# Moving the third round of decays and the third group of tiles behind the first inversion in a fused RWKV-7 and hash-routing kernel

## The chip, the cores and the metric

The kernel runs on one core of one Trainium2 chip. The metric is the device time of one execution in microseconds (us). A core has a matrix engine (PE, with its weight loads shown as PEld), a vector engine (DVE), an activation engine (ACT), a general engine (POOL), and SyncE (SP), which here only issues DMAs. Each engine works through its own queue in order.

## The reference

The first block is a recurrent attention (RWKV-7) over 4 batches, 8 heads, 768 steps and a head size of 40. The second block sends each of the 3072 resulting rows (320 wide) to one of 8 experts, chosen by a hash of its token id.

```python
for t in range(S):                      # B, H, S, D = 4, 8, 768, 40
    y[:, :, t] = einsum('bhd,bhde->bhe', r[t], state)
    Sa = einsum('bhde,bhe->bhd', state, a[t])
    state = state * w[t][:, :, None, :] - einsum('bhd,bhe->bhde', Sa, b[t])
    state = state + einsum('bhd,bhe->bhde', v[t], k[t])
x = y.transpose(0, 2, 1, 3).reshape(B * S, H * D)
expert = token_ids * 2654435761 % 8
for e in range(8):                      # w1: 320x1024, w2: 1024x320
    out[expert == e] = maximum(x[expert == e] @ w1[e], 0) @ w2[e]
```

## The kernel before

**The work.** The sequence is cut into 12 chunks of 64 steps. A *tile* is one chunk of two batches, so there are 24 tiles, numbered u = 0 to 23; tiles u and u + 2 are the same batches and hang together through the state. Everything is float32.

- `decays(ri, ...)` makes the running products of `w` for one *round* of two chunks, which is four tiles: round ri serves tiles 4ri to 4ri + 3, and there are 6 rounds. It loads `wt` (L352), multiplies up a tree (`todo`, L363/L366, DVE), joins the halves by a small matmul `f_ps` (L382, PE), and spreads products and reciprocals down the tree (`then`, L389 to L377, DVE). The results `pb` and `qb` are stored to DRAM by 8 DMAs on SP (L337); tiles read them back as `pl` and `ql` through POOL's queue (L458, L460). Round 0 is turned on DVE and read without that detour.
- `tile_a(u)` loads `al` and `kb` (inputs a, b, k; SP, L308), forms `at` and `z` (DVE, L473 and L477), transposes them (`z_ps` L491 and `t_ps` L528 on PE, copied by ACT) and makes the scores `a_ps` (PE). ACT copies the part to be inverted to `pk` and `no`; DVE masks the rest into `mk` (L521).
- `group_i(gi, ...)` inverts the scores of four tiles at once, on DVE alone: POOL clears `nu` (L546), DVE transposes `pk` into it (L552), then runs 30 pairs of `outer` (L570) and `nu` (L577), and transposes the result into `ut` (L585, L586). There are six groups; "inversion 0" is that of tiles 0 to 3.
- `tile_m(u)` finishes the inverse on PE and ACT (`x_ps`, `u_ps`), and `tile_b(u)` does the recurrent part: `r0` and `r1` (`r_ps`), `nc`, `x_t`, `s` (state update, DVE `st`), `sd`, `rc` (DVE mask `mr`, L700), and `y` (DVE `xs`, L736), which POOL stores to `x_rows` (L740).
- `routing()` sorts the tokens to experts, in 30 small steps; the expert part (L1003 `up_ps`, L1021 `dn_ps`) follows when all tiles are done.

**The order.** The queues of PE, DVE, ACT and POOL are written out by hand. Each piece is given a *tick*; all pieces are sorted by tick and issued in that order, so a tick is a place in the queue and not a time. `tile_a(u)` stands at tick u, `tile_m(u)` at u + 7, `tile_b(u)` at u + 8 (`LAG = 8`), its `y` at u + 9. Within a tick the steps follow the list `STEPS`, a step being 1/14 of a tick. Inversion gi starts behind the scores of its last tile (tick 4gi + 3.8) and must be done at tick 4gi + 7.2, just before `tile_m` of its first tile. SP's queue is not in that list (`manual_schedule(engines={PE, DVE, Activation, Pool})`): the framework orders the DMAs issued there.

Buffers limit how early a load may start: `al`, `kb`, `pl`, `ql` have two each, `wt` one. A load into a buffer that is still being read holds up whatever stands behind it in its queue.

Of the kernel before, what the change touches and what calls it, by code (L numbers as in the profile page):

```python
# [36 lines left out]
F32 = mybir.dt.float32  # L37
# [10 lines left out]
def kernel(  # L48
# [55 lines left out]

    col = const.tile([P, P], I32)
    nc.gpsimd.iota(col[:], pattern=[[1, P]], base=0, channel_multiplier=0)
    row = const.tile([P, P], I32)
# [14 lines left out]


    FH = F // 2
    early = pool("early", 1)

    def load_w1(t, e, dma):

# [36 lines left out]
    plan = []  # L165


    STEPS = ["r0", "r1", "z", "y", "nc", "x", "at_t", "x_t", "s", "u", "sd", "a", "r_t", "rc"]

    def at_tick(tick, step=None, order=0):  # L170
        if step is not None:
# [83 lines left out]
    def half(i):  # L255
        return slice(i * C, (i + 1) * C)
# [58 lines left out]
    def decays(ri, t_w, t0, span, t_f, span_f=None, stores=None):  # L315
# [28 lines left out]

        @at_tick(t_w)
        def _():
            x["w"] = wt = early.tile([P, HC * D], F32, tag="wt", name="wt")

            dma = (nc.sync.dma_start, nc.scalar.dma_start if ri < 2 else nc.sync.dma_start)
            for y in range(2 * RN):  # L350
                src = w.rearrange("b h (n t) e -> (b h) n (t e)", t=HC)[:, ri * 2 * RN + y]
                dma[y % 2](wt[y * BH:(y + 1) * BH], src)  # L352
# [87 lines left out]
    def of_batches(rows, b0, n):  # L440
        return rows[:, b0 * H:(b0 + n) * H, :].rearrange("t bh e -> t (bh e)")

    def tile_a(u):

        n, g = divmod(u, NG)
        ri, rn = divmod(n, RN)
        x = tiles[u]

        @at_tick(u - 1.7)
        def _():  # L450
            x["p"] = pl = work.tile([P, DM], F32, tag="pl", name="pl")
            x["a"] = al = work.tile([P, DM], F32, tag="al", name="al")
            x["q"] = ql = work.tile([P, 2, DM], F32, tag="ql", name="ql")
            x["kb"] = kb = work.tile([P, 2, DM], F32, tag="kb", name="kb")
            p_rows, q_rows = ((rounds[0][i].rearrange("t (bh e) -> t bh e", e=D) if ri == 0 else pq_dram[ri]["pq".index(i)])
                              [rn * C:(rn + 1) * C] for i in "pq")
            for be in range(2):
                nc.gpsimd.dma_start(pl[half(be)], of_batches(p_rows, 2 * g + be, 1))  # L458
            for be in range(2):
                nc.gpsimd.dma_start(ql[half(be)], of_batches(q_rows, 2 * g, 2))  # L460
            load(lambda be, rows: by_head(al, rows), a, 2 * g, n * C)
# [5 lines left out]
        late = {4: 0.45, 5: 0.3, 6: 0.15}.get(u, 0.0)  # L467

        @at_tick({0: -0.6, 1: -0.4, 2: 0.45, 3: 1.45}.get(u, u + late - (0.1 if late else 0.6)))
        def _():  # L470
            x["at"], x["z"] = at_r(u), z_r(u)

            nc.vector.scalar_tensor_tensor(wide(x["at"]), by_head(x["a"]), -1.0, by_head(x["p"]), op0=OP.mult, op1=OP.mult)  # L473

            def view(t):
                return t.rearrange("p b (hp two e) -> p (b hp) two e", hp=HP, two=2)
            nc.vector.tensor_tensor(heads(x["z"].rearrange("p b hp x -> p (b hp) x")), view(x["kb"][:]), view(x["q"][:]),  # L477
                                    op=OP.mult)

        @at_tick(u + late, "at_t")  # L480
        def _():
            x["at_t"] = t = work.tile([P, HP, 2, C], F32, tag="at_t", name="at_t", bufs=LAG)
            turn(t, x["at"])

        @at_tick(u + late, "z")
        def _():
            x["z_t"] = t = z_t
            p = two_banks("z_ps")
            for be in range(2):
                for hp in range(HP):  # L490
# [46 lines left out]
    def group_i(gi, t0, t1, t2):  # L537
# [22 lines left out]
        for j in range(1, BLK - 1):  # L560

            m = BLK - 1 - j
            full = [P, j // 2 + 1, m, 2]
            n = full[1] * m * 2

            @at_tick(t1 + dt * (2 * j - 1), order=9)
            def _(j=j, full=full, n=n):
                x["t"] = work.tile([P, BLK * BLK // 4 + BLK // 2], F32, tag="outer", name="outer")
                tv = x["t"][:, 0:n].rearrange("p (c i k) -> p c i k", c=full[1], k=2)
                nc.vector.tensor_tensor(tv, paired(x["u"])[:, 0:full[1], j:j + 1, :].to_broadcast(full),  # L570
                                        paired(x["n"])[:, j // 2, j + 1:, j % 2].unsqueeze(1).unsqueeze(3).to_broadcast(full),
                                        op=OP.mult)
# [72 lines left out]
    def tile_b(u, t0):  # L645
# [2 lines left out]
        last = n == NCH - 1  # L648
        st, sb, sd = st_r(g), sb_r(g), sd_r(g)

        @at_tick(t0, "r0")
        def _():
            x["r1_ps"] = p = bank([P, DM], "r1_ps").rearrange("p (two x e) -> p two x e", two=2, e=D)
            for _, be, hp in heads_of("hq", "be", "al"):
                mm(p[half(al(hp)), :, hp % HQ * 2 + be, :], x["at_t"][:, hp, be, :], sb[:, be, hp],
                   start=be == 0 and hp % HQ == 0, stop=False)
# [97 lines left out]
    t_a = STEPS.index("a") / len(STEPS)  # L754

    decays(0, -4.0, -3.0, 0.4, -2.5, 0.3)
    decays(1, -2.15, -1.9, 0.4, (-0.55, -0.54, -0.53, -0.35, -0.34, -0.3, -0.29, 0.2), stores=1.34)
    decays(2, -0.25, 0.87, 0.45, (1.87, 1.9, 1.91, 2.0, 2.01, 2.1, 2.11, 2.2), stores=3.34)
    for ri in range(3, NR):
        t0 = ri * RN * NG - 5.0  # L760
        decays(ri, t0 - 1.0, t0 + 0.25, 1.0, t0 + 1.3, 1.1)
    for u in range(NU):
        tile_a(u)
        tile_s(u, u + LAG)
        tile_m(u, u + LAG)
# [13 lines left out]
    def routing():  # L779
# [4 lines left out]
        for b_ in range(B):  # L784
# [475 lines left out]
```

## Time and profile before

| what | value |
|---|---|
| median of 3 runs | 657.6 us (655.33 to 657.83) |
| the profiled execution: time / span | 660.41 us / 658.5 us |
| busy: PE, DVE, ACT, POOL | 560.7, 349.4, 295.0, 194.8 us |
| start of inversion 0 and end of its last transpose | 57.5 and 93.8 us |
| end of inversions 1, 2, 3, 4, 5 | 143.7, 205.3, 257.6, 309.6, 360.3 us |
| start of the expert part | 410.0 us |
| mean granted PE clock | 0.946 |

The time of an execution is 1.9 us above its span. The expert part from 410 us on is untouched by the diff. The page's second part cuts the span into 40 slices of 16.5 us; each digit is a busy share in tenths.

### The profile page before, as it was taken

Reading aid. Unit: us, or ns where it says so; the run is one execution under the profiler, and the core shown is the slowest. Engines: PE = TensorE matmul, PEld = TensorE weight load, DVE = VectorE, ACT = ScalarE, POOL = GpSimd, SP = SyncE. Lnnn points to the kernel's source line nnn. Section 1 sums busy time; section 2 is a strip of 40 time slices with the busy share of each in tenths; the row PEclk is TensorE's granted clock in tenths of the full one; section 3 lists DMA queues with packets and bytes.
Section 4 is the critical chain, followed back from the end, with each engine's and each line's share of the span. In section 5 each row is a group of like instructions: output and inputs, shape, how many; then the busy total and the mean of one; then the engine's idle time right before and its main releaser. Section 6 shows DMA issues by size and latency. Waiting matters only on the chain.

```text
span 658.5 us, 22965 instructions
## 1 busy us (share of the span) xinstructions
PE 560.7 (85%) x9866; PEld 427.1 (65%) x9866; DVE 349.4 (53%) x920; ACT 295.0 (45%) x695; POOL 194.8 (30%) x327
## 2 busy tenths in 40 slices
PE   0244559979998999999979998999999999999995
PEld 0233447868887887888868877775665646565653
DVE  6766968957868996796698723133020302113010
ACT  4133447757776677768746662113131313101110
POOL 0503341325343343533312330173404131212101
PEclk9967669979999999999997998999999999999999
DMA  5999996878598787842422640869243364131000
GB/s 90 203 174 170 180 185 119 162 152 158 117 192 153 142 166 140 184 96 54 98 51 50 162 106 17 275 216 313 74 144 117 104 219 143 38 101 40 30 11 24
DMA packets 195770, 85.13 MB, mean 129 GB/s; under 512 B 176718, under 2 KB 186191, under 8 KB 195664
## 3 DMA queue, kind: packets, MB, share of 16 engines
q1 hardware_dynamic: 184208, 46.25, 36.5%
q0 software_dynamic: 11264, 36.72, 19.3%
q8 instruction: 78, 1.28, 0.8%
q10 hardware_dynamic: 192, 0.66, 0.4%
q14 instruction: 28, 0.23, 0.1%
HBM read 66.54 MB, written 15.40 MB: 124 GB/s over the span
## 4 chain that ended last, share of the span: by engine, by line
PE 44%; issue 22%; DVE 19%; DMA 6%; POOL 4%; ACT 3%; SPq 1%; POOLq 0%; DVEq 0%; ACTq 0%
PE up_ps L1003 6%; PE dn_ps L1021 6%; PE y_ps L289 4%; DVE nu L577 3%; PE s_ps L289 3%; DVE outer L570 3%; PE a_ps L289 3%; PE r_ps L289 3%; PE x_t_ps L688 3%; PE rc_ps L289 2%; POOL out_dram L1026 2%; PE t_ps L528 2%; DVE mr L700 2%; PE z_ps L491 2%; PE nc_ps L289 2%
## 5 line engine op out<-in xcount | busy, mean ns | idle before, releaser
L1011 DVE TENSOR_SCALAR ht<-up_ps 128x416 f32<-128x416 f32 (+2 forms) x36 | 19.4, 543 | 165.0 <-PE up_ps L1008 163.4
L1021 PE MATMUL dn_ps<-w,ht 128*128 128x320 f32 x336 | 91.7, 433 | 0.0
L1003 PE MATMUL up_ps<-xt,w 128*128 128x416 f32 x224 | 81.3, 516 | 0.0
L1021 PEld LDWEIGHTS dn_ps<-w,ht 128*128 128x128 f32 x336 | 63.3, 190 | 25.5
L1026 POOL DMA_INDIRECT out_dram<-o,idx_all x26 | 26.1, 1006 | 166.5 <-ACT o L1025 160.4
L740 POOL DMA_DIRECT2D x_rows<-xs x44 | 23.3, 534 | 171.5 <-DVE xs L736 101.5
L1003 PEld LDWEIGHTS up_ps<-xt,w 128*128 128x128 f32 x224 | 41.9, 190 | 36.9 <-issue 31.7
L570 DVE TENSOR_TENSOR outer<-nu 128x252 f32<-128x252 f32 (+8 forms) x180 | 63.3, 352 | 4.6
L577 DVE TENSOR_TENSOR nu<-nu,outer 128x252 f32<-128x252 f32 (+8 forms) x180 | 63.4, 352 | 4.3
L1013 ACT ACTIVATE ht<-up_ps 128x416 f32<-128x416 f32 (+2 forms) x36 | 17.2, 479 | 107.4 <-PE up_ps L1008 107.4
L1025 ACT COPY o<-dn_ps 128x320 f32<-128x320 f32 x26 | 11.1, 425 | 92.0 <-PE dn_ps L1021 92.0
L491 PE MATMUL z_ps<-ident,z 128*104 128x128 f32 x192 | 32.8, 326 | 20.7 <-DVE z L477 17.5
L493 ACT COPY z_t<-z_ps 104x512 f32<-104x512 f32 x48 | 25.8, 589 | 54.8 <-PE z_ps L491 54.8
L491 PEld LDWEIGHTS z_ps<-ident,z 128*104 128x104 f32 x192 | 25.6, 155 | 23.5 <-issue 18.3
L458 POOL DMA_DIRECT2D pl<-p_rows x48 | 25.3, 532 | 52.2 <-DVE at L473 21.5
L678 ACT COPY x<-nc_ps 64x320 f32<-64x320 f32 x48 | 20.2, 420 | 38.9 <-PE nc_ps L289 38.4
L289 PE MATMUL a_ps<-at_t,z_t 64*64 64x64 f32 x1536 | 30.9, 233 | 7.5 <-ACT at_t L529 7.3
L700 DVE TENSOR_TENSOR mr<-rc_ps,after 128x1024 f32<-128x1024 f32 x24 | 29.3, 1219 | 14.9 <-PE rc_ps L289 14.8
L289 PEld LDWEIGHTS a_ps<-at_t,z_t 64*64 64x64 f32 x1536 | 27.3, 145 | 12.8 <-ACT at_t L529 9.8
L289 PE MATMUL rc_ps<-r_t,x_t 64*64 64x64 f32 x1536 | 30.2, 226 | 5.1 <-issue 4.4
L289 PE MATMUL y_ps<-z,mr 128*64 128x40 f32 x768 | 27.3, 231 | 7.2 <-DVE mr L700 6.8
L289 PEld LDWEIGHTS rc_ps<-r_t,x_t 64*64 64x64 f32 x1536 | 26.2, 138 | 10.0 <-issue 6.4
(227 smaller groups left out, 1123.9 us busy)
## 6 DMA issues: line engine op xcount, KB each, us to landing
ql<-q_rows POOLq DMA_DIRECT2D x48, 160.0 KB, 5.2
w<-in_moe_w_dram SPq DMA_DIRECT2D x10, 640.0 KB, 6.9
w<-in_moe_w_dram SPq DMA_DIRECT2D x10, 512.0 KB, 4.5
al<-in_a_dram SPq DMA_DIRECT2D x48, 80.0 KB, 4.4
kb<-in_b_dram SPq DMA_DIRECT2D x48, 80.0 KB, 3.8
kb<-in_k_dram SPq DMA_DIRECT2D x48, 80.0 KB, 3.9
pl<-p_rows POOLq DMA_DIRECT2D x48, 80.0 KB, 4.2
r<-in_r_dram SPq DMA_DIRECT2D x48, 80.0 KB, 3.6
```

The costliest lines, as they stand in the source:

```text
L289: nc.tensor.matmul(out_, lhsT=lhsT, rhs=rhs, start=start, stop=stop, skip_group_check=True)
L458: nc.gpsimd.dma_start(pl[half(be)], of_batches(p_rows, 2 * g + be, 1))
L491: nc.tensor.transpose(p[0:R, be, hp * P:(hp + 1) * P], x["z"][:, be, hp, :], ident[:])
L493: nc.scalar.copy(t[0:R, be].rearrange("p h t -> p (h t)"), p[0:R, be])
L570: nc.vector.tensor_tensor(tv, paired(x["u"])[:, 0:full[1], j:j + 1, :].to_broadcast(full), paired(x["n"])[:, j // 2, j + 1:, j % 2].unsque ...
L577: nc.vector.tensor_tensor(o, o, x["t"][:, 0:n].rearrange("p (c i k) -> p c i k", c=full[1], k=2), op=OP.add)
L678: nc.scalar.copy(x["x"][half(be), be].rearrange("p (a q) (two e) -> p a (q two) e", a=2, two=2)[:, :, :, 0:D], p[half(be), :, 0:HP * D].re ...
L700: nc.vector.tensor_tensor(t[:].rearrange("p two h t -> p (two h) t"), p[:].rearrange("p two (h t) -> p (two h) t", t=C), after[:].unsqueez ...
L740: dma(x_of[2 * g + be, n * C:(n + 1) * C], xs[half(be), :])
L1003: nc.tensor.matmul(p[:], lhsT=w1[c][:, (f0 + i) * P:(f0 + i + 1) * P], rhs=xt[:, c, 0:n], start=(c == 0), stop=False)
L1021: nc.tensor.matmul(p[i * m:(i + 1) * m], lhsT=ht[:, f, c0:c0 + m], rhs=w2[f // (FP // 2)][:, f % (FP // 2), :], start=(f == 0), stop=(f == ...
L1026: st = nc.gpsimd.indirect_dma_start(out=out[:], out_offset=bass.IndirectOffsetOnAxis(ap=idx, axis=0), in_=o[0:m], in_offset=None, bounds_c ...
```

## The change

- **Order of the rounds and tiles.** `t_of(u)` gives the tick of `tile_a(u)`. Tiles 4 to 6 stay late by 0.45, 0.3 and 0.15 as before. Tiles 8 to 11 move from ticks 8 to 11 to ticks 10.4, 10.85, 11.3 and 11.75; tiles 12 and 13 move by 0.5 and 0.2. Inversion gi begins behind the scores of its last tile at the new tick and is due at the same tick as before, so inversion 2 begins at 12.6 and not at 11.9.
- **Decays.** Round 2 is computed at ticks 7.2 to 8.1 (before: 0.87 to 2.2), round 3 at 8.6 to 10.4 (before: 7.25 to 9.4). `wt` has two buffers, and the loads of rounds 1, 3, 4 and 5 are issued earlier (4 and 5 by 1.6 ticks).
- **First inputs.** `al` and `kb` have a piece of their own. For tiles 0 to 3 it stands at ticks -3.9 to -2.7; tiles 2 and 3 borrow the buffers of `x_t`, `mr` and `py`, which are not needed before tick 8.
- **`r0`** of the next tile moves from the head of a tick to between `r_t` and `rc` at its end, just behind the scores.
- **Room.** `outer` has one buffer in place of two; `row` and the temporaries of `routing()` share buffers that are free by then.
- **Routing.** The last steps are spread over ticks 27.25 to 30.3 (before: 27.35 to 29.1), and the first two gathers move from tick 29.2 to 30.5.

```diff
-    STEPS = ["r0", "r1", "z", "y", "nc", "x", "at_t", "x_t", "s", "u", "sd", "a", "r_t", "rc"]
+    STEPS = ["r1", "z", "y", "nc", "x", "at_t", "x_t", "s", "u", "sd", "a", "r_t", "r0", "rc"]
...
-            x["w"] = wt = early.tile([P, HC * D], F32, tag="wt", name="wt")
+            x["w"] = wt = early.tile([P, HC * D], F32, tag="wt", name="wt", bufs=2)
...
+    LATE = {4: 4.45, 5: 5.3, 6: 6.15}
+    CLOSE = {8: 10.4, 9: 10.85, 10: 11.3, 11: 11.75}
+    AFTER = {12: 12.5, 13: 13.2}
+
+    def t_of(u):
+        return {**LATE, **CLOSE, **AFTER}.get(u, u)
...
-        @at_tick(u - 1.7)
+        ta, close = t_of(u), u in CLOSE
+        @at_tick(ta - 1.7)
...
+        @at_tick({0: -3.9, 1: -3.8, 2: -2.8, 3: -2.7}.get(u, ta - 1.69))
+        def _():
+            kb_tag = {2: "x_t", 3: "mr"}.get(u)
...
+            x["a"] = al = work.tile([P, DM], F32, tag="py" if kb_tag else "al", name="al")
             load(lambda be, rows: by_head(al, rows), a, 2 * g, n * C)
...
-        @at_tick({0: -0.6, 1: -0.4, 2: 0.45, 3: 1.45}.get(u, u + late - (0.1 if late else 0.6)))
+        @at_tick({0: -0.6, 1: -0.4, 2: 0.45, 3: 1.45}.get(u, ta - (0.1 if u in LATE else 0.4 if close else 0.6)))
...
-        @at_tick(u + late, "at_t")
+        @at_tick(ta + 0.43 if close else ta, None if close else "at_t")
...
-        @at_tick(u + late, "z")
+        @at_tick(ta + 0.4 if close else ta, None if close else "z")
...
-        @at_tick(u + late, "a")
+        @at_tick(ta, "a")
...
-                x["t"] = work.tile([P, BLK * BLK // 4 + BLK // 2], F32, tag="outer", name="outer")
+                x["t"] = work.tile([P, BLK * BLK // 4 + BLK // 2], F32, tag="outer", name="outer", bufs=1)
...
-        @at_tick(t0, "r0")
+        @at_tick(t0 - 1, "r0")
...
-    decays(1, -2.15, -1.9, 0.4, (-0.55, -0.54, -0.53, -0.35, -0.34, -0.3, -0.29, 0.2), stores=1.34)
-    decays(2, -0.25, 0.87, 0.45, (1.87, 1.9, 1.91, 2.0, 2.01, 2.1, 2.11, 2.2), stores=3.34)
-    for ri in range(3, NR):
+    decays(1, -2.9, -1.9, 0.4, (-0.55, -0.54, -0.53, -0.35, -0.34, -0.3, -0.29, 0.2), stores=1.34)
+    decays(2, -0.25, 7.2, 0.3, 7.5, 0.6)
+    decays(3, 5.0, 8.6, 0.8, 9.4, 1.0)
+    for ri in range(4, NR):
         t0 = ri * RN * NG - 5.0
-        decays(ri, t0 - 1.0, t0 + 0.25, 1.0, t0 + 1.3, 1.1)
+        decays(ri, t0 - 2.6, t0 + 0.25, 1.0, t0 + 1.3, 1.1)
...
-        t0 = gi * GRP + GRP - 1 + t_a
-        group_i(gi, t0 + 0.05, t0 + 0.1, t0 + 3.4)
+        t0 = t_of(gi * GRP + GRP - 1) + t_a
+        group_i(gi, t0 + 0.05, t0 + 0.1, (gi + 2) * GRP - 0.81)
...
+    ROWS_IN = 3
     for i in range(30):
-        t = 4.5 if i < 1 else NU + 3.35 + 0.105 * (i - 12) if i > 11 else NU - 0.25 + 0.3 * i
+        t = 4.5 if i < 1 else NU - 0.25 + 0.3 * i
+        if 12 <= i < 12 + 5 * ROWS_IN:
+
+            t = NU + 3 + (i - 12) // 5 + (0.25, 0.3, 0.65, 0.66, 1.05)[(i - 12) % 5]
+        elif i >= 12 + 5 * ROWS_IN:
+            t = NU + 3 + ROWS_IN + 0.1 + 0.12 * (i - 12 - 5 * ROWS_IN)
...
-    @at_tick(last_u + LAG + 2, "y", order=-1)
+    @at_tick(NU - 1 + LAG - 0.5)
```

More of the change, by code (lines that the diff above doesn't have):

```diff
@@ L106 @@
     nc.gpsimd.iota(col[:], pattern=[[1, P]], base=0, channel_multiplier=0)
-    row = const.tile([P, P], I32)
+    early = pool("early", 1)
+    row = early.tile([P, P], I32, tag="nu", name="row")
     nc.gpsimd.iota(row[:], pattern=[[0, P]], base=0, channel_multiplier=1)
@@ L114 @@
     nc.vector.memset(ones[:], 1.0)
+    bj = route.tile([P, 1], F32)
+    nc.vector.tensor_scalar(bj[:], row[:, 0:1], 1.0, None, op0=OP.add)
     WP = 8
@@ L124 @@
     FH = F // 2
-    early = pool("early", 1)
     def load_w1(t, e, dma):
@@ L447, in tile_a @@
         x = tiles[u]
-        @at_tick(u - 1.7)
+        ta, close = t_of(u), u in CLOSE
+        @at_tick(ta - 1.7)
         def _():
             x["p"] = pl = work.tile([P, DM], F32, tag="pl", name="pl")
-            x["a"] = al = work.tile([P, DM], F32, tag="al", name="al")
             x["q"] = ql = work.tile([P, 2, DM], F32, tag="ql", name="ql")
-            x["kb"] = kb = work.tile([P, 2, DM], F32, tag="kb", name="kb")
             p_rows, q_rows = ((rounds[0][i].rearrange("t (bh e) -> t bh e", e=D) if ri == 0 else pq_dram[ri]["pq".index(i)])
@@ L460, in _ @@
                 nc.gpsimd.dma_start(ql[half(be)], of_batches(q_rows, 2 * g, 2))
+        @at_tick({0: -3.9, 1: -3.8, 2: -2.8, 3: -2.7}.get(u, ta - 1.69))
+        def _():
+            kb_tag = {2: "x_t", 3: "mr"}.get(u)
+            if kb_tag:
+                kb = work.tile([P, 2 * HP * P], F32, tag=kb_tag, name=f"kb_{kb_tag}", bufs=1)[:, 0:2 * DM].rearrange("p (b x) -> p b x", b=2)
+            else:
+                kb = work.tile([P, 2, DM], F32, tag="kb", name="kb")[:]
+            x["kb"] = kb
+            x["a"] = al = work.tile([P, DM], F32, tag="py" if kb_tag else "al", name="al")
             load(lambda be, rows: by_head(al, rows), a, 2 * g, n * C)
@@ L464, in _ @@
             load(lambda be, rows: by_head(kb[:, be], rows), k, 2 * g, n * C, crossed=True)
-        late = {4: 0.45, 5: 0.3, 6: 0.15}.get(u, 0.0)
-        @at_tick({0: -0.6, 1: -0.4, 2: 0.45, 3: 1.45}.get(u, u + late - (0.1 if late else 0.6)))
+        @at_tick({0: -0.6, 1: -0.4, 2: 0.45, 3: 1.45}.get(u, ta - (0.1 if u in LATE else 0.4 if close else 0.6)))
         def _():
@@ L476, in view @@
                 return t.rearrange("p b (hp two e) -> p (b hp) two e", hp=HP, two=2)
-            nc.vector.tensor_tensor(heads(x["z"].rearrange("p b hp x -> p (b hp) x")), view(x["kb"][:]), view(x["q"][:]),
+            nc.vector.tensor_tensor(heads(x["z"].rearrange("p b hp x -> p (b hp) x")), view(x["kb"]), view(x["q"][:]),
                                     op=OP.mult)
-        @at_tick(u + late, "at_t")
+        @at_tick(ta + 0.43 if close else ta, None if close else "at_t")
         def _():
@@ L791, in routing, with part_of, by_e @@
         nc.vector.tensor_scalar(eid[:], tok[:, :, 0], E - 1, None, op0=OP.bitwise_and)
-        mine = route.tile([P, E, TPP], F32)
+        ET_ = E * TPP
+        large = early.tile([P, HC * D], F32, tag="wt", name="large", bufs=2)
+        def part_of(i, n=1):
+            return large[:, i * ET_:(i + n) * ET_]
+        def by_e(v):
+            return v.rearrange("p (e c) -> p e c", e=E)
+        mine = by_e(part_of(0))
         nc.vector.tensor_tensor(
-            mine[:], eid[:].unsqueeze(1).to_broadcast([P, E, TPP]),
+            mine, eid[:].unsqueeze(1).to_broadcast([P, E, TPP]),
             iota_e[:].unsqueeze(2).to_broadcast([P, E, TPP]), op=OP.is_equal)
         yield
-        mflat = mine[:].rearrange("p e c -> p (e c)")
+        mflat = part_of(0)
         sums_ps = bank([P, 2, E * TPP], "sums_ps")
@@ L800, in routing @@
         nc.tensor.matmul(sums_ps[:, 1, :], lhsT=upper[:], rhs=mflat, start=True, stop=True)
-        sums = route.tile([P, 2, E * TPP], F32)
-        nc.scalar.copy(sums[:], sums_ps[:])
+        sums = part_of(1, 2).rearrange("p (two x) -> p two x", two=2)
+        nc.scalar.copy(sums, sums_ps[:])
         yield
-        rst = route.tile([P, E, TPP], F32, name="rst", tag="sel")
-        nc.vector.memset(rst[:], 1.0)
+        rst = by_e(part_of(4))
+        nc.vector.memset(rst, 1.0)
         nc.vector.memset(rst[:, :, 0:1], 0.0)
-        cum = route.tile([P, E, TPP], F32)
-        cumf = cum[:].rearrange("p e c -> p (e c)")
-        nc.vector.tensor_tensor_scan(cumf, rst[:].rearrange("p e c -> p (e c)"), sums[:, 0, :], 0.0,
+        cumf = part_of(3)
+        cum = by_e(cumf)
+        nc.vector.tensor_tensor_scan(cumf, part_of(4), sums[:, 0, :], 0.0,
                                      op0=OP.mult, op1=OP.add)
@@ L818, in of_token @@
         def of_token(dst, src):
-            sel = route.tile([P, E, TPP], F32, name="sel", tag="sel")
-            nc.vector.tensor_tensor(sel[:], mine[:], src, op=OP.mult)
-            nc.vector.tensor_reduce(dst, sel[:].rearrange("p e c -> p c e"), axis=AX.X, op=OP.add)
+            sel = by_e(part_of(4))
+            nc.vector.tensor_tensor(sel, mine, src, op=OP.mult)
+            nc.vector.tensor_reduce(dst, sel.rearrange("p e c -> p c e"), axis=AX.X, op=OP.add)
         rank = route.tile([P, TPP], F32)
-        of_token(rank[:], cum[:])
+        of_token(rank[:], cum)
         yield
@@ L868, in routing @@
         nc.vector.tensor_scalar(key_i[:], key_i[:], P.bit_length() - 1, None, op0=OP.logical_shift_right)
-        bj = route.tile([P, 1], F32)
-        nc.vector.tensor_scalar(bj[:], row[:, 0:1], 1.0, None, op0=OP.add)
         yield
```

## The prediction, made before the changed kernel ran

> **What bounds the kernel now.** I read the 40 slices first.
>
> ```profile
> PE   0244559979998999999979998999999999999995
> DVE  6766968957868996796698723133020302113010
> PEclk9967669979999999999997998999999999999999
> DMA  5999996878598787842422640869243364131000
> ```
>
> PE is at 2 to 5 tenths for six slices (to 99 us) and near 9 from then on. So time is to be had before 99 us, and work moved from there lands where PE and DVE are both full. Busy time by stretches says how full (columns: busy us of PE, PEld, DVE, ACT, POOL, then granted clock, DMA share, GB/s).
>
> ```profile
> 57.50:94.00 36.50, 15.81 (x270) 13.69 (x270) 31.28 (x77) 12.88 (x29) 10.62 (x22) 0.61 1.01 176
> 104.00:117.00 13.00, 12.13 (x386) 10.46 (x382) 12.48 (x36) 8.99 (x24) 1.04 (x2) 1.00 0.54 89
> 117.00:131.00 14.00, 13.01 (x392) 11.44 (x387) 13.46 (x32) 10.49 (x26) 5.22 (x11) 1.00 0.83 162
> ```
>
> In inversion 0 the DMA engines never rest (1.01) and DVE works 31.3 of 36.5 us; in the ticks behind it PE and DVE both work over 90%. Then the timeline, for what delays inversion 0 and where the later ones stand:
>
> ```profile
> 36.59 1.16 PE L289 MATMUL a_ps<-at_t,z_t 64*64 64x64 f32 x64 [1.73 <-ACT at_t L529]
> 37.59 0.83 DVE L477 TENSOR_TENSOR z<-kb,ql 128x640 f32<-128x640 f32 x1 [1.97 <-DMA kb<-in_k_dram]
> 41.55 0.49 DVE L366 TENSOR_TENSOR pb<-wt 128x320 f32<-128x320 f32 x1 [2.54 <-DMA wt<-in_w_dram]
> 44.10 0.65 PE L382 MATMUL f_ps<-own,partner 128*128 128x40 f32 x2 [6.35 <-DVE own L363]
> 48.62 1.99 PE L289 MATMUL a_ps<-at_t,z_t 64*64 64x64 f32 x64 [0.93 <-ACT at_t L529]
> 54.03 1.16 PE L289 MATMUL a_ps<-at_t,z_t 64*64 64x64 f32 x64 [1.21 <-ACT at_t L529]
> 57.46 1.24 DVE L552 STREAM_TRANSPOSE nu<-pk 128x1024 f32<-128x1024 f32 x1
> 85.93 0.83 DVE L477 TENSOR_TENSOR z<-kb,ql 128x640 f32<-128x640 f32 x1 [3.00 <-DMA kb<-in_k_dram]
> 92.61 1.20 DVE L586 STREAM_TRANSPOSE ut<-nu 128x1024 f32<-128x1024 f32 x1
> 142.50 1.20 DVE L586 STREAM_TRANSPOSE ut<-nu 128x1024 f32<-128x1024 f32 x1
> 157.03 1.24 DVE L552 STREAM_TRANSPOSE nu<-pk 128x1024 f32<-128x1024 f32 x1
> 204.10 1.20 DVE L586 STREAM_TRANSPOSE ut<-nu 128x1024 f32<-128x1024 f32 x1
> ```
>
> The scores of tiles 1, 2, 3 come at 36.59, 48.62, 54.03. Between the first two stands round 2's `f_ps` in PE's queue; it waits for DVE, which waits for `wt`. Inversions end at 93.8, 143.7 and 205.3.
>
> **The sum, stage by stage,** on the profiled execution (660.41 us). A minus is time won.
>
> *To the start of inversion 0.* Round 2's decays leave; so does the wait for `kb`, now loaded at once. Tile 1 followed tile 0 by 36.59 - 32.25 = 4.34 us, the pace of PE, ACT and PE again. Tiles 2 and 3 at that pace score at 40.93 and 45.27; from the last score to L552 is 57.46 - 54.03 = 3.43. Start 48.70: **-8.8**. Tile 0 wins nothing: DVE saves 2.78 us of waiting for round 1's `wt`, but `z` also needs `ql`, issued by 22.2 with a median of 5.2 to landing, and began at 27.22. POOL must clear `nu` by then, behind tile 4's `pl` and `ql`, which wait for round 1's stores; those were issued from 41.54 to 49.4, behind 2.9 us of `wt` and 3 us of inputs on SP, and their data are ready at 33.1 and 35.2, so some 43 and a clear at about 47 should do.
>
> *Inversion 0.* The 3.00 us at 85.93 is a load behind others. Round 2's stores leave: 8 x 1024 packets at 18.2 ns (74.9% of 16 engines over 40 us for 26355 packets) on 16 engines are 9.3 us of full DMA. **-3.0**, end at 82.0. One buffer for `outer` costs nothing: the three instructions sharing it already depend on each other in one queue; a semaphore instead would show as gaps.
>
> *Inversion 1 (ticks 7.2 to 11.2).* Before: 143.70 - 93.81 = 49.9 us, DVE idle 3.62 and 2.31, so 44.0 of DVE. In come round 2's decays: tree 2.50 (41.55 to 44.05), joining 0.96, spreading 4.34 (46.85 to 51.19), together 7.8. Out go `at` and `z` of tile 11 and two `mk`: 1.1 + 1.2. That is 49.5. PE loses two tiles' scores (2.6 each: `z_ps` 1.0, `t_ps` 0.5, `a_ps` 1.1), so it has under 45 and waits at `y` for `mr`: DVE is the bound. With 3.6 idle for tile 7's `mk` again and 2.0 for one late `z` it is 55.1: **+5.2**, end at 137.1. Queued behind a late `z` is the rest of the inversion, and behind that PE's `x_ps`.
>
> *The crowd (ticks 11.2 to 12.5).* Inversion 2 needs tile 11's scores, and PE has three tiles' scores and 1.2 ticks of recurrence ahead of them. By start-to-start times between 146 and 158 us: x 0.63, x_t 0.88, s 1.37, u 0.62, sd 0.82, r_t 0.58, r0 0.60, rc 1.1, r1 0.65, y 1.6, nc 0.60, x 0.63, x_t 0.88, and scores: 17.3. PE may begin 1.2 before the second transpose ends; behind the last score 3.43 - 1.16 = 2.3 pass. PE comes from waiting: after its 3.75 us stall at 141.6 `z_ps` took 1.95, not 1.08, at a granted 0.52. I add 1.0 for that (bounds 0 and 1.7). 19.4 against 157.03 - 143.70 = 13.3: **+6.1**, start 156.5. The Trainium skill ("TensorE: Matmul & The Clock Gate", section "What's actually happening") says that an idle window of about 3.4 us halves PE's clock until as long a stretch is busy. It speaks against this change, whose new waits sit in PE's queue; three such waits would be an estimated 5.1 us by it, were PE the bound there.
>
> *Inversion 2.* Before 205.30 - 157.03 = 48.3, idle 0.41, 0.93, 4.71. DVE content 42.2, less `mr` 1.13, `xs` 0.41 and early decays 0.7, now ahead of it, is 40.0. I keep the 4.71, a `z` whose inputs stood behind round 4's stores on SP, and drop the small ones, as PE has less per tick: 44.7, **-3.6**, end at 201.2.
>
> *From there* both orders have the same work. `r0` ahead of `rc` leaves less between `rc` and `y`: where no `z_ps` lies between, 0.55 + 0.56 = 1.1, while `mr` needs 0.24 + 1.22: 0.4 a tick in the three ticks before the last, +1.2 (bounds 0 and eight ticks, 3.2). Spread routing spares PE waits of 0.32 and 0.31 at `tok_ps`: -0.6. The later gathers (then about 392 us, 3.0 to land) are wanted at 406; if late they would show there. The `wt` loads issued earlier (four DMAs, 2.9 us of SP each) pass ahead of tiles' inputs; the second buffer lets them start, and the 2.0 above covers a late input. **+0.6**.
>
> Sum: -8.8 - 3.0 + 5.2 + 6.1 - 3.6 + 0.6 = **-3.5**: 656.9 in a profiled execution. That execution was 2.8 above the median, so 657.6 - 3.5 = **654.1**.
>
> **Rivals.**
> - *The front is kept:* the crowd overlaps and DVE finds room, so only -11.8 + 0.6 counts: 646.4. For it: PE does the same work, and idled some 61 of the first 94 us. Against: DVE's 49.5.
> - *Slower: the crowd runs at the startup's pace.* Four tiles 0.45 tick apart pass through one `z_t`, two PSUM pairs and ACT. Tile 3 followed tile 2 by 5.41 us at a low clock; against 2.6 in my sum that is 2.8 x 3 = +8.4, so +4.9: 662.5. It decides once inversion 2 starts 3.5 us later than 156.5. For it: ACT has 18 us of copies there. Against: PE has recurrence between, which the startup lacked.
> - *The start is not freed:* SP leaves round 1's stores late, POOL's clear ends at 55.4 as before, and the first stage gives 2.0 in place of 8.8: +3.3, 660.9.
>
> **How the numbers follow.** What I forecast 0.48 (650 to 659: the idle on DVE 3 us either way), the front kept 0.22, the crowd 0.20, the start not freed 0.10. A measurement tells about 0.5%, 3.3 us: faster is below 654.3, slower above 660.9. The forecast lies at that edge: 0.28 faster, 0.20 same. The front kept: faster. The crowd: 0.18 slower, 0.02 same. The last: halves. Together 0.50, 0.27, 0.23. The range takes in the rivals: 645 to 663, with about 1 in 10 left out above and less below.
>
> **What would show it.** L552 first at 48 to 50 (55 or more: start not freed); the first `ut` done at 82; the second at 135 to 139, with PE waiting for `mr` in between; inversion 2 from 156 (160 or more: the crowd); its end at 201. I am wrong if PE stays above 9 tenths through inversion 1, or if DVE waits over 5 us for inputs in ticks 9 to 13.

## The result, and the profile after

The changed kernel takes **678.96 us** (median of 4 runs, 674.49 to 681.50) against 657.72 us before, a ratio of 1.032 (95% interval 1.026 to 1.038). It is slower by 21 us, and the forecast of 654.1 with its range to 663 was wrong. The execution that was profiled took 674.49 us (span 672.7), the shortest of the four; the stages below add up to 14 us against the profile of before, so some 7 us of the difference between the medians lie outside what these two profiles can show.

The slices of the page after, with the same rows as before:

```profile
PE   0263675888798998999898998999999999999995
DVE  6648878963798796687578743331130302023010
PEclk9995676879999999999988999999999999999999
DMA  8998839599888697672322542659352455131000
```

A slice is now 16.8 us. PE starts earlier, but from 84 to 185 us it is at 5 to 8 tenths, where before it was near 9 from 99 us on; its clock is at 6 to 8 tenths until 151 us, and DMA is at 9 from 135 to 168 us (before 7 and 8). The timeline at the points that the prediction named (start, duration, and in brackets the idle time ahead and its releaser):

```profile
28.90 0.83 DVE L495 TENSOR_TENSOR z<-kb,ql 128x640 f32<-128x640 f32 x1 [4.70 <-DMA ql<-q_rows]
51.53 1.23 DVE L570 STREAM_TRANSPOSE nu<-pk 128x1024 f32<-128x1024 f32 x1
85.71 1.20 DVE L604 STREAM_TRANSPOSE ut<-nu 128x1024 f32<-128x1024 f32 x1
143.72 0.69 DVE L539 TENSOR_TENSOR mk<-a_ps,after 128x512 f32<-128x512 f32 x1 [3.58 <-ACT no L537]
146.64 1.20 DVE L604 STREAM_TRANSPOSE ut<-nu 128x1024 f32<-128x1024 f32 x1
172.85 1.23 DVE L570 STREAM_TRANSPOSE nu<-pk 128x1024 f32<-128x1024 f32 x1
214.13 1.20 DVE L604 STREAM_TRANSPOSE ut<-nu 128x1024 f32<-128x1024 f32 x1
```

Inversion 0 starts at 51.5 (48.7 was forecast), inversion 1 ends at 147.8 (137.1), inversion 2 starts at 172.9 (156.5). The windows of inversion 0, inversion 1, the crowd behind it and inversion 2 (us; busy PE, PEld, DVE, ACT, POOL; granted clock, DMA share, GB/s):

```profile
51.50:86.90 35.40, 16.39 (x269) 14.28 (x269) 31.07 (x77) 12.82 (x28) 6.40 (x13) 0.55 0.79 128
86.90:147.80 60.90, 47.43 (x1135) 41.41 (x1134) 47.13 (x130) 30.13 (x76) 18.70 (x36) 0.78 0.70 131
147.80:172.80 25.00, 22.26 (x634) 19.07 (x633) 9.69 (x25) 19.55 (x46) 14.50 (x28) 0.99 1.02 191
172.80:215.30 42.50, 35.79 (x1040) 31.40 (x1039) 38.80 (x96) 27.76 (x68) 11.40 (x22) 0.96 0.82 151
```

DVE has 47.1 us of work in an inversion 1 of 60.9, and its waits there add up to 11.7 us, where the sum had 5.6. By stages, from such windows; the last two columns are two of the experiments below (E2: `r0` moved alone; E4: `r0` back and no stores of round 3):

| stage (us) | forecast | before | after | measured | E2 | E4 |
|---|---|---|---|---|---|---|
| start of inversion 0 | -8.8 | 57.5 | 51.5 | -6.0 | 50.4 | 51.0 |
| inversion 0 | -3.0 | 36.3 | 35.4 | -0.9 | 32.9 | 32.9 |
| inversion 1 | +5.2 | 49.9 | 60.9 | +11.0 | 55.7 | 54.1 |
| crowd, to the start of inversion 2 | +6.1 | 13.3 | 25.0 | +11.7 | 29.0 | 21.8 |
| inversion 2 | -3.6 | 48.3 | 42.5 | -5.8 | 40.5 | 40.9 |
| from there to the expert part | +0.6 | 204.7 | 208.6 | +3.9 | 205.4 | 203.6 |
| sum | -3.5 | 410.0 | 423.9 | +13.9 | 413.9 | 404.3 |

The stages miss the forecast by 2.8, 2.1, 5.8, 5.6, -2.2 and 3.3 us, 17.4 in all: no single stage holds the miss.

### The profile page after: what moved, and what is told of

Read it like the earlier page. It is cut to its first block, busy times and chain, and to the rows that moved or that the text cites. A ratio compares the mean times of both kernels' runs of the same rounds, so it can differ in the third digit from the quotient of the medians.

```text
span 672.7 us, 22958 instructions
## 1 busy us (share of the span) xinstructions
PE 567.1 (84%) x9866; PEld 432.2 (64%) x9866; DVE 350.3 (52%) x920; ACT 294.9 (44%) x695; POOL 194.0 (29%) x327
## 4 chain that ended last, share of the span: by engine, by line
PE 42%; issue 21%; DVE 18%; ACT 6%; DMA 5%; POOL 5%; SPq 3%; POOLq 0%; DVEq 0%; ACTq 0%
PE up_ps L1034 6%; PE dn_ps L1052 6%; PE y_ps L291 4%; PE s_ps L291 4%; PE x_t_ps L706 3%; PE a_ps L291 3%; DVE nu L595 3%; DVE outer L588 3%; SPq L310 3%; DVE mr L718 3%; POOL out_dram L1057 2%; PE x_ps L291 2%; PE z_ps L509 2%; PE sd_ps L766 2%; PE nc_ps L291 2%
## 5 line engine op out<-in xcount | busy, mean ns | idle before, releaser
L1042 DVE TENSOR_SCALAR ht<-up_ps 128x416 f32<-128x416 f32 (+2 forms) x36 | 19.4, 543 | 165.0 <-PE up_ps L1039 163.4
L291 PE MATMUL y_ps<-z,mr 128*64 128x40 f32 x768 | 28.8, 236 | 22.5 <-DVE mr L718 22.2
L509 PEld LDWEIGHTS z_ps<-ident,z 128*104 128x104 f32 x192 | 25.5, 154 | 26.4 <-issue 21.8
L291 PEld LDWEIGHTS y_ps<-z,mr 128*64 128x64 f32 x768 | 26.4, 145 | 24.9 <-DVE mr L718 24.6
L291 PE MATMUL a_ps<-at_t,z_t 64*64 64x64 f32 x1536 | 32.5, 241 | 10.0 <-ACT at_t L547 7.7
L539 DVE TENSOR_TENSOR mk<-a_ps,after 128x512 f32<-128x512 f32 x24 | 16.6, 691 | 46.3 <-ACT no L537 46.3
L291 PEld LDWEIGHTS a_ps<-at_t,z_t 64*64 64x64 f32 x1536 | 28.8, 153 | 14.8 <-ACT at_t L547 10.2
L718 DVE TENSOR_TENSOR mr<-rc_ps,after 128x1024 f32<-128x1024 f32 x24 | 29.2, 1219 | 15.4 <-PE rc_ps L291 15.4
```

The source lines that it names most:

```text
L291: nc.tensor.matmul(out_, lhsT=lhsT, rhs=rhs, start=start, stop=stop, skip_group_check=True)
L718: nc.vector.tensor_tensor(t[:].rearrange("p two h t -> p (two h) t"), p[:].rearrange("p two (h t) -> p (two h) t", t=C), after[:].unsqueez ...
```

## The experiments

All ratios are to the kernel before on the same chip, with the 95% interval.

**E1. The parts.** Each of these undoes or does one part. The first keeps everything but the move of tiles and rounds:

```diff
-    CLOSE = {8: 10.4, 9: 10.85, 10: 11.3, 11: 11.75}
-    AFTER = {12: 12.5, 13: 13.2}
+    CLOSE = {}
+    AFTER = {}
...
     # round 2's and round 3's decays at their ticks of before
```

> All of the change but the move: tiles 8 to 13 and the decays of rounds 2 and 3 stand at their old ticks; early inputs, second wt buffer with earlier loads, r0 ahead of rc, one outer buffer and the spread routing stay. If the move is what costs (the theory), inversion 1 lasts 50 us as before and not 61, inversion 2 starts 13 us behind it and not 25, and some of the front is still won: 648 to 657 us. If r0 or the earlier wt loads cost (rivals), it stays above 663 us.

Measured: 662.39 us, 1.006 (1.002 to 1.011), between the two ranges. The move of tiles is no more than part of the loss: a kernel without it is still slower than before.

The second is the kernel before with the move alone, and one `wt` buffer, so that round 3's `wt` is loaded at tick 8.2:

```diff
+    LATE, CLOSE, AFTER, t_of(u)                  # as in the change, with all that uses them
-    decays(2, -0.25, 0.87, 0.45, (1.87, 1.9, 1.91, 2.0, 2.01, 2.1, 2.11, 2.2), stores=3.34)
+    decays(2, -0.25, 7.2, 0.3, 7.5, 0.6)
+    decays(3, 8.2, 8.6, 0.8, 9.4, 1.0)
```

> The kernel before with the move alone: tiles 8 to 13 and the decays of rounds 2 and 3 at their new ticks; inputs, r0, routing and one wt buffer as before (round 3's wt is loaded at tick 8.2, behind round 2's tree). If the move is what costs: inversion 1 near 60 us and inversion 2 starting 20 us or more behind it, 668 to 682 us. If r0, the wt loads or the routing cost: 648 to 658 us, since the start is freed of round 2.

Measured: 681.29 us, 1.036 (1.028 to 1.044), the slowest of all. DVE waits 8.30 us for `wt` at 113.95, inside inversion 1, and inversion 2 starts at 183.3. Without the second `wt` buffer the move starves its own decays; so this says what the buffer is worth to the move, and not what the move costs in the change; the time lies in the range named for the move, but for this reason. Inversion 0 starts at 52.8 us here, against 57.5 before, with the inputs loaded as before.

The third puts back the list of steps and the place of `r0`:

```diff
-    STEPS = ["r1", "z", "y", "nc", "x", "at_t", "x_t", "s", "u", "sd", "a", "r_t", "r0", "rc"]
+    STEPS = ["r0", "r1", "z", "y", "nc", "x", "at_t", "x_t", "s", "u", "sd", "a", "r_t", "rc"]
...
-        @at_tick(t0 - 1, "r0")
+        @at_tick(t0, "r0")
```

> The change with r0 put back to the head of its tick (the list of steps too). The theory gives r0 nothing: within 4 us of the changed kernel, 674 to 683 us, and y still waits over 15 us for mr. If r0 behind the scores makes y wait for mr (rival): 655 to 668 us, and that wait falls to the 7 us of before.

Measured: 662.72 us, 1.010 (1.007 to 1.013). Two lines of the change, priced at +1.2 in the sum, are worth 1.032 - 1.010 = 2.2%, some 15 us; the expectation that they are worth nothing fell. Inversion 1 is 54.2 us here, against 55.1 forecast.

The fourth computes round 2's decays in the start again, with tiles 8 to 11 still late:

```diff
-    decays(2, -0.25, 7.2, 0.3, 7.5, 0.6)
+    decays(2, -0.25, 0.87, 0.45, (1.87, 1.9, 1.91, 2.0, 2.01, 2.1, 2.11, 2.2), stores=3.34)
```

> The change with round 2's decays back at ticks 0.87 to 2.2 (its wt now has a buffer of its own); tiles 8 to 13 stay at their new ticks. If the 7.8 us of DVE work brought into inversion 1 are the larger part of the cost: inversion 1 at 53 us or less, total 664 to 671 us. If the late tiles are: inversion 1 at 57 or more, total 673 to 682 us.

Measured: 673.26 us, 1.019 (1.009 to 1.028). Inversion 0 starts at 51.9, as in the change (51.5), so with the early inputs the start is free even with the decays in it. The second kernel has the decays out and the inputs as before, and starts at 52.8. Either step alone wins 3.6 to 5.6 us of the start (the front alone, below, starts at 53.9), and both together 6.0 in the change: they do not add. Inversion 1 is 57.3, only 3.7 shorter, although DVE's work in it fell from 47.1 to 40.6 us: DVE waits 14.9 us there, against 11.7 in the change.

The same two lines of `r0` on the kernel before, and then the change without the move and without `r0`:

```diff
-    STEPS = ["r0", "r1", ...                      # on the kernel before
+    STEPS = ["r1", ..., "r_t", "r0", "rc"]
-        @at_tick(t0, "r0")
+        @at_tick(t0 - 1, "r0")
...
+    CLOSE = {}, AFTER = {}, rounds 2 and 3 as before, STEPS and "r0" as before   # on the change
```

> The kernel before with nothing but r0 moved behind the scores. Theory now: r0 between r_t and rc costs each tick about 0.2 us of PE (r0 to rc is 0.70 us from start to start and not 0.60, and so on) and up to 0.5 of waiting for mr, so 24 to 32 ticks give +8 to +16: 666 to 674 us, and rounds behind inversion 2 last 54 to 55.5 us and not 52.3. Rival, that r0 only hurts where the moved tiles have put DVE out of step: within 3 us of before, 655 to 661.

> The change without the move and without r0's move: early inputs, two wt buffers with earlier loads, spread routing, shared room. If move and r0 are the two costs and they add: 662 less 8 to 12, so 650 to 655 us, faster than the kernel before. If r0 costs only together with the move: 659 to 664.

Measured: 661.92 us, 1.010 (1.005 to 1.015) for the edit of `r0` on the kernel before, just above the rival's range. **653.59 us, 0.994 (0.991 to 0.997)** for the front alone (early inputs, two `wt` buffers, spread routing), as expected: this one beats both kernels, the one before by 0.6%. It starts inversion 0 at 53.9 and inversion 2 at 149.3.

The routing by itself, on the kernel before:

```diff
+            t = NU + 3 + (i - 12) // 5 + (0.25, 0.3, 0.65, 0.66, 1.05)[(i - 12) % 5]
...
-    @at_tick(last_u + LAG + 2, "y", order=-1)
+    @at_tick(NU - 1 + LAG - 0.5)
```

> The kernel before with only the last routing steps spread over the ticks and the first two gathers later. Theory: of the 3.5 to 4 us that the front-only version wins, the stage from the last inversion to the expert part holds most (46.2 us against 49.7), so this alone gives about 653 to 655, with that stage at 46 to 47 us. Rival: that stage moved because the stage before it was changed, and routing gives the 0.6 us of my sum: about 657, and the gain belongs to the early inputs and the second wt buffer.

Measured: 658.38 us, 1.001 (0.997 to 1.005). It is worth nothing that can be measured; the rival is right that the front's gain belongs to the inputs and the buffer, which were not parted.

**E2. What the edit of `STEPS` does.** A step's tick is its index over 14. With `r0` taken from the head of the list and put near its end, every other step but `rc` comes one place, 0.071 of a tick, earlier (they are twelve; the expectations below count one too few). The pieces with plain ticks (`at`, `z`, the last transposes of an inversion) do not, and an inversion's pairs do so in part: `t_a`, the place of `a` in the list, sets the tick of the first pair, and a plain tick that of the last. So DVE's queue is another one in the change than in the third experiment, although `r0` runs on PE. `mk` of tiles 4 and 5, made during inversion 0, now stands *ahead* of the next tile's `at` and `z`. At the other tiles that order is the old one, but `mk`, `mr`, `st` and `xs` change places with pairs of the inversion, with decays, and `xs` with its last transposes. Two causes were mixed, and these kernels part them. The first moves `r0` with the old list, the second keeps the new list and puts `r0` back:

```diff
+    STEPS = ["r0", "r1", "z", "y", "nc", "x", "at_t", "x_t", "s", "u", "sd", "a", "r_t", "rc"]
+        @at_tick(t0 - 1 + 12.5 / len(STEPS))          # first: r0 alone
...
+        @at_tick(t0 - 0.01)                           # second: the shift alone, list as in the change
```

> The change, with the list of steps as before and r0 given the tick between r_t and rc by number: r0 stands where the change has it in PE's queue, and DVE's and ACT's queues are those of the kernel with r0 back (662.7 us). Theory A, the shift of the other eleven steps is what costs: 662 to 666, inversion 1 at 54 to 56 us (after: 60.9), steady rounds at 52 to 53 us. Theory B, the later rc and mr are what costs: 675 to 679, inversion 1 at 60, y waiting over 20 us for mr.

> The change, with r0 put back behind rc by number and the new list of steps kept: the other steps stay a fourteenth of a tick early, DVE's and ACT's queues are those of the change, PE's queue has r0 in its old place beside r1. Theory A: 675 to 679 as after, inversion 1 at 60 us, DVE waiting for the scores at mk over 40 us in all. Theory B: 662 to 666.

Measured: `r0` alone 665.65 us, 1.007 (1.003 to 1.011); the shift alone **679.73 us, 1.028 (1.023 to 1.033)**. Theory A holds for the time: the move of `r0` costs nothing that can be told (1.007 against 1.010 with `r0` back), and the shift costs 1.028 - 1.010 = 1.8% with `r0` back and 1.032 - 1.007 = 2.5% with `r0` moved, 12 to 17 us. Two of its numbers missed: the shift alone is just above its 675 to 679, and the first steady round of the `r0` kernel took 55.3 us, not 52 to 53. The timeline of inversion 0 shows the mechanism there. The change:

```profile
64.49 0.69 DVE L539 TENSOR_TENSOR mk<-a_ps,after 128x512 f32<-128x512 f32 x1 [1.14 <-ACT no L537]
65.43 0.48 DVE L491 SCALAR_TENSOR_TENSOR at<-al,pl 128x320 f32<-128x320 f32 x1
65.83 0.82 DVE L495 TENSOR_TENSOR z<-kb,ql 128x640 f32<-128x640 f32 x1
66.80 1.92 PE L509 MATMUL z_ps<-ident,z 128*104 128x128 f32 x8 [4.00 <-DVE z L495]
```

and the kernel with `r0` alone:

```profile
62.14 0.48 DVE L491 SCALAR_TENSOR_TENSOR at<-al,pl 128x320 f32<-128x320 f32 x1
62.55 0.82 DVE L495 TENSOR_TENSOR z<-kb,ql 128x640 f32<-128x640 f32 x1
63.28 0.69 DVE L539 TENSOR_TENSOR mk<-a_ps,after 128x512 f32<-128x512 f32 x1
```

In the change DVE stands at `mk` for scores that PE and ACT are still making, and the next tile's `at` and `z`, which need nothing from them, queue behind. So PE waits longer for `z` (4.00 us against 2.21, and 3.94 against 2.95 at the next tile), and its next scores are late again. With `at` and `z` ahead, `mk` finds its scores done and does not wait. DVE's waits at `mk` in inversion 0 are 1.14, 0.21 and 0.96 us in the change and none with `r0` alone, close to the 2.5 us of the stage. The granted clock does not part the two kernels there (0.55 in the change, 0.50 with `r0` alone).

In inversion 1 `mk` changes no place with an `at` or `z`, and the loss is larger. Summed over it, DVE waits 11.7 us in the change (7.2 of them at `mk`, 3.0 at `st`) and 6.6 with `r0` alone, and PE waits at `y` for `mr` 9.5 us (6.79 and 2.70) and 4.64; either difference is about that of the stage (60.9 against 55.7). The first `mk` of the stage stands ahead of four spreading steps of the decays in the change and waits 3.60 us, not 2.21. The last stands one instruction of the inversion earlier, and `xs` is ahead of the transposes. In the change, then with `r0` alone:

```profile
143.72 0.69 DVE L539 TENSOR_TENSOR mk<-a_ps,after 128x512 f32<-128x512 f32 x1 [3.58 <-ACT no L537]
```

```profile
136.07 0.69 DVE L539 TENSOR_TENSOR mk<-a_ps,after 128x512 f32<-128x512 f32 x1 [0.62 <-PE y_ps L291]
105.39 1.94 PE L291 MATMUL y_ps<-z,mr 128*64 128x40 f32 x32 [4.64 <-DVE mr L718]
```

What each of these exchanges costs was not measured; only the shift as a whole was. The waits of DVE at `mk` over the whole program (us in total, times, longest), for the shift alone, then for `r0` alone:

```profile
DVE mk L539 <- ACT no L537: 48.7, 21, 4.2
```

```profile
DVE mk L539 <- ACT no L537: 36.7, 14, 4.5
```

The same test without the move of tiles, `r0` by number in the front-only version, and the steps moved half a place the *other* way in that version:

```diff
+        @at_tick(t0 - 1 + 12.5 / len(STEPS))                              # r0 alone
...
+            tick += (STEPS.index(step) + 0.5) / len(STEPS)                # half a place later
```

> The front-only version (653.6 us) with r0 moved by number and the list of steps as before. With the list changed the same kernel took 662.4. Theory A: the shift made most of the 8.8 us, and r0 by itself costs 0 to 3.5 us (dearer ticks of 0.16 us in 20 ticks): 653 to 657. Theory B: 661 to 663.

> The front-only version (653.6 us) with every step half a place (a twenty-eighth of a tick) later against the pieces with plain ticks: mk, mr and xs come one instruction of the inversion later in DVE's queue. If early mk and mr cost time by waiting in DVE's queue, a little later should save some of it: 649 to 653. If the list before is already late enough, there is nothing to win, or y waits longer for mr: 653 to 657.

Measured: 654.45 us, **0.989 (0.986 to 0.993)** with `r0` alone, where the list edit gave 1.006: the shift also makes the first experiment slow. Half a place later gives 662.12, 1.000 (0.996 to 1.004), against 0.994 without it. The theory that later is better found no support. The loss is nearly all in the start: inversion 0 begins at 63.0 instead of 53.9, and the way from there to the expert part is 348.6 against 346.7. Tile 0's scores began at 38.4, not 33.2. By the half place `at_t` of tile 0 comes to tick 0.464, behind `at` of tile 2 at 0.45, which is written into the same one of two buffers:

```profile
36.57 1.11 PE L546 MATMUL t_ps<-ident,at 128*128 128x128 f32 x4 [5.24 <-DVE at L491]
```

It waits for that `at`, and by the order of the queue it is tile 2's values that it transposes. The same holds for tiles 1 and 3. So this kernel is no clean test of the theory; behind the start it shows no gain.

**E3. The inputs in the crowd.** The crowd of `r0` alone is longer than the change's own (29.0 against 25.0 in the table), though the whole is shorter. So there is a second limit. The third kernel of E1, which has the same queue on DVE, shows it:

```profile
142.18 0.49 DVE L491 SCALAR_TENSOR_TENSOR at<-al,pl 128x320 f32<-128x320 f32 x1 [2.67 <-DMA al<-in_a_dram]
152.14 0.49 DVE L491 SCALAR_TENSOR_TENSOR at<-al,pl 128x320 f32<-128x320 f32 x1 [4.63 <-DMA al<-in_a_dram]
156.46 0.82 DVE L495 TENSOR_TENSOR z<-kb,ql 128x640 f32<-128x640 f32 x1 [3.83 <-DMA ql<-q_rows]
146.92 1.04 POOL L469 DMA_DIRECT2D ql<-q_rows  x2 [11.22 <-DVE mk L539]
141.86 3.35 SPq L339 DMA_DIRECT2D q_rows<-qb  x4
```

SP issues without a pause from 133 to 150 us. Round 3's stores of `qb` (the last line, 3.35 us of issuing) stand between the inputs of two tiles. Tile 12 is the first to read round 3's rows; POOL's queue holds its `ql` for 11.2 us, so everything behind it is late. The profile names DVE as what ended this wait; in the change the same load waits 12.5 us for the stores of `q_rows`, and in E4, which has none, it does not wait. Tile 12's `at` and `z` stand ahead of tile 10's `mk` in DVE's queue, and DVE waits 13 us for inputs in the crowd (2.67, 4.63, 3.83 above and 1.84 for a `kb`).

First, the tree and the spreading of round 3 half a tick to one tick sooner, so that the stores are out before (with `r0` back):

```diff
-    decays(3, 5.0, 8.6, 0.8, 9.4, 1.0)
+    decays(3, 5.0, 8.12, 0.5, 8.65, 0.6)
```

> The change with r0 back, and with round 3's decays at ticks 8.1 to 9.25 and not 8.6 to 10.4, the same work on DVE, so that its stores are issued ahead of the inputs of tiles 10 and 11. If the crowd waits for inputs because SP holds round 3's stores behind them and POOL's q load waits for the stores (theory): from the end of inversion 0 to the start of inversion 2 it is 80 us or less in place of 86, total 653 to 659. If the crowd is bound by PE and ACT (the rival of the prediction): 84 us or more, total 660 to 667.

Measured: 663.01 us, 1.011 (1.006 to 1.016). The crowd shrank from 32.1 to 23.0 us, and inversion 1 grew from 54.2 to 59.7: mostly moved, and nothing won in the time.

**E4.** Then without the stores:

```diff
-            elif stores is None:
+            elif stores is None and ri != 3:
...
-            pq_dram[ri]
+            pq_dram[2 if ri == 3 else ri]           # where tiles 12 to 15 read
```

> The change with r0 back, and without round 3's stores: its 8 DMAs are left out and tiles 12 to 15 read round 2's rows. Same work on PE, DVE and ACT. Theory (inputs): DVE no longer waits 4 us for a q load, 72 to 79 us from the end of inversion 0 to the start of inversion 2, total 648 to 656. If PE and ACT bind the crowd: 84 us or more, total 659 or more.

Measured: 654.33 us, 1.000 (0.996 to 1.003), against 1.010 with them. From the end of inversion 0 to the start of inversion 2 it takes 75.8 us, where my sum had 55.1 + 19.4 = 74.5 and the kernel with the stores 86.2. It is close to what the sum described, but it leaves out work that the kernel needs.

**E5.** The same with the change's list of steps:

> The change as it is (r0 between the scores), with round 3's eight stores left out and tiles 12 to 15 reading round 2's rows; so it is the run without round 3's stores (654.3 us) plus the move of r0. r0 cost 4.7 to 6.6 us on the kernel before, 8.8 us in the kernel without the move, and 16 us in the changed kernel. Theory A: r0's price is its own, a later rc mask and dearer ticks, and does not hang on the late inputs; then the step from 654.3 is 16 us again, to about 670, and the steady rounds (end of inversion 2 to end of inversion 3) stay at 55 us against 52. Theory B: the part above 5 to 9 us came of the late inputs, which stall PE and halve its clock; then about 660 to 663, with inversion 1 at 55 us and not 61.

Measured: 677.15 us, 1.031 (1.025 to 1.036). This is theory A, and more than its 670: the list edit costs 3.1% here (1.031 - 1.000), some 20 us (23 by the medians), against 2.2% with the stores; that the two differ is at the edge of the intervals. Seen the other way, leaving the stores out wins 1.0%, some 7 us, with the old list, and nothing that can be told with the new one (1.031 against 1.032). The windows of the crowd show it more clearly, this kernel's first, then that of E4:

```profile
147.90:171.20 23.30, 22.13 (x635) 19.00 (x634) 9.49 (x24) 19.59 (x46) 10.44 (x20) 0.98 0.85 166
```

```profile
138.00:159.80 21.80, 20.55 (x598) 17.90 (x597) 10.27 (x28) 18.39 (x44) 11.48 (x22) 1.00 0.88 171
```

With the shift inversion 1 ends 10 us later, the inputs have landed by then (DVE waits for none in this crowd, and 3.45 us in the change's), and PE works 22.1 of 23.3 us: PE's work is nearly the whole of the crowd, and the stores add little to it (25.0 us with them, 22.3 of it PE's work). Without the shift the inputs are the limit, and taking the stores away lowers it to PE's.

**E6.** Last, the stores kept, but issued from ACT's queue in one piece at tick 10.42, with `r0` by number:

```diff
-                nc.sync.dma_start(pq_dram[ri][i]...
+                (nc.scalar if ri == 3 else nc.sync).dma_start(pq_dram[ri][i]...
...
+    decays(3, 5.0, 8.6, 0.8, 9.4, 1.0, stores=10.42)
```

> The change with r0 moved by number (665.7 us, 1.0069 of before), and round 3's eight stores issued from ACT's queue in one piece at tick 10.42, in place of SP's. The bytes are the same; SP no longer has 4.7 and 3.6 us of stores between the inputs of tiles 9 to 12. Theory A, SP's order and issue time hold up the inputs: the start of inversion 2 comes 5 to 8 us sooner against the end of inversion 1, and the time is 657 to 661. Theory B, the DMA engines' bytes hold them up (their share there was 1.02): 663 to 668, with the waits for al, kb and ql moved and not gone. ACT pays its own time for eight issues (on SP each took about 1 us), up to 8 us off its own 32 of 55 in that stage, which has room.

Measured: 670.43 us, 1.015 (1.010 to 1.019), outside both. The crowd fell from 29.0 to 22.1, as theory A had it, and inversion 1 grew from 55.7 to 67.9:

```profile
130.40 7.90 ACTq L339 DMA_DIRECT2D q_rows<-qb  x4
138.34 1.07 ACT L708 COPY x_t<-x_t_ps 128x512 f32<-128x512 f32 x2 [13.30 <-DMA al<-in_a_dram]
139.47 1.95 PE L509 MATMUL z_ps<-ident,z 128*104 128x128 f32 x8 [12.73 <-ACT x_t L708]
```

ACT's copy of `x_t` stood 13.3 us behind the stores, and PE waited 12.7 for it. My allowance of "up to 8 us, with room" took ACT's time as a sum, while it was a wait in a queue. Since the inputs also had 12 us longer to land, this run does not settle whether SP's order, the bytes, or the wait of tile 12's `ql` for the stores holds them up; that stays open.

## Why the prediction was wrong, point by point

- **What failed first is the term "From there", in which `r0` was priced.** It followed `r0` on PE, between `rc` and `y`, and got +1.2 (bounds 0 and 3.2). For `r0` itself that holds: no cost that could be told on either base. But the edit changes the list of steps, and the list sets the ticks of twelve other steps and the start of each inversion's pairs. The sum had no term for `mk`, `mr`, `xs` and `st` moving against pairs, decays, `at` and `z`: it put that at nothing without a reason. It costs 12 to 17 us, and some 20 where no late input held the crowd up. In the table, after against E2, it appears as 2.5 us in inversion 0, 5.2 in inversion 1, 2.0 in inversion 2 and 3.2 behind it, with 4.0 won back in the crowd, and not in the ticks for which `r0` was priced. Why it costs is shown for inversion 0; for the rest only the waits are.
- **Inversion 1, +5.2:** with the shift undone +4.2 to +5.8 in the two last columns, so the DVE sum was right: with `r0` alone the stage less DVE's waits is 49.1 us, against 49.5. The sign named for it (DVE bound, PE waiting for `mr`) was half seen: `y` waited 6.79 and 2.70 us for `mr` in the change, but DVE itself waited 11.7 us.
- **Crowd, +6.1:** the stage was mis-sized, and a wait was left out. I summed PE's instructions from 1.2 us before the second transpose ends to the last score, 17.3 plus 1.0, and 2.3 behind it. In E4, where little else holds them, they took 18.8 with 1.2 of waiting, and 3.0 behind: 21.8 against 19.4, so the sum of work was about right. In the change itself they took 20.0 with 2.55 of waiting (1.74 for `sd`, 0.81 for `mr`), and 3.6 behind: 25.0. What the sum left out was SP's and POOL's queues: moved tiles load their inputs just where round 3 is stored. With the stores and the old list the stage takes 32.1 us (third kernel of E1), so that is worth 10.3 us of the stage and 1.0% of the time; in the change the shift hides most of it (25.0 against 23.3 without the stores). The sign that I gave, over 5 us of DVE waiting for inputs, came up with 13 us in the third kernel; in the change's crowd it was 3.45. I had allowed 2.0.
- **The rival "crowd at the startup's pace"** named a stage that did lose, and its sign came up (inversion 2 from 172.9, more than 3.5 after 156.5), but partly by luck: 10.7 of these 16.4 us were lost before the crowd began. Its reason is not borne out: ACT was busy 19.6 of 25.0 us there, and with the inputs on time and the old list PE, not ACT, was nearly full.
- **Inversion 0 and its start, -8.8 and -3.0:** the start gave -6.0. I had credited it to the decays' leaving and the early `kb`; either alone gave most of what was won (52.8 and 51.9 in E1). Tile 0's `z` came at 28.90, not at 27.22, after 4.70 us for `ql`. The first slice of DMA rose from 5 to 8 tenths, by the inputs and `wt` issued at once; that `ql` is late for that reason is only argued, and I had put it at nothing. Inversion 0 gave -0.9 with the shift and -3.4 without.
- **Inversion 2, -3.6:** -5.8 and, without the shift, -7.4 to -7.8: better than the sum. I had kept a wait of 4.71 us for `z`; DVE waits 1.7 us in all in the stage after the change, and none of it for an input.
- **The rest, routing -0.6:** no gain that can be told.

With both failed terms taken out of the kernel (E4) the result is 654.3 us, and the forecast was 654.1. That they agree so closely is luck: E4's stages miss the sum by 2.3, -0.4, -1.0, 2.4, -3.8 and -1.7 us, which in part cancel, and against the kernel before on the same chip it is 1.000, where the forecast was a gain of 0.5%. It also shows that, even without the work of the stores, this reordering wins less than the inputs and the buffer alone, at 0.994, or 0.989 with `r0` moved by number.

## What to carry to other kernels

Where order comes from positions in a list, an edit of the list moves everything in it: compare the queues of *every* engine before and after, and price each pair that changes places, above all one that puts a waiting instruction ahead of independent work. When tiles are moved, write out SP's and POOL's queues at the new place as carefully as PE's; the sum of the busiest compute engine is only a lower bound there. And two delays do not add where one hides the other, so the removal of one may show nothing until the other is gone, as with the stores here.

## What the runs showed of the hardware

The clock fell after waits that were shorter than I had reckoned with. In the change, PE's timeline:

```profile
110.44 1.94 PE L291 MATMUL y_ps<-z,mr 128*64 128x40 f32 x32 [6.79 <-DVE mr L718]
126.17 1.13 PE L291 MATMUL y_ps<-z,mr 128*64 128x40 f32 x32 [2.70 <-DVE mr L718]
143.15 1.88 PE L291 MATMUL y_ps<-z,mr 128*64 128x40 f32 x32
```

The same 32 matmuls took 1.94 us behind a wait of 6.79, 1.13 behind one of 2.70, and 1.88 when PE had idled 2.28 us shortly before (at 139.3 to 141.6). The granted clock was 0.50 from 110 to 116 us and, after the idle of 2.28, from 141.6 to 147. After the wait of 2.70 it was 1.00 and 0.98 until 128, and then 0.50 until 131, with PE at work all the while. So the length of a wait alone did not decide, and here the lower clock came some 2 us after the wait had ended. The Trainium skill ("TensorE: Matmul & The Clock Gate", section "What's actually happening") gives about 3.4 us of idleness for the halving; the first row agrees with it, and the halvings after 2.70 and 2.28 us do not by themselves.

The issue of round 3's four `q_rows` stores took 3.35 us on SP (`r0` alone) and 7.90 us on ACT (E6), that of the four `p_rows` stores 4.68 us on SP and 4.76 on ACT; no run here shows why they differ.
